# K's logarithm and exponential in one row on ScalarE, the next norm behind them, and the copy and subtraction of x behind those and behind Q's products

## The chip, the cores and the metric

The kernel runs on one core of a Trainium2 chip. The metric is device microseconds of one execution on that core. PE is TensorE (matmuls; PEld is its weight load), DVE is VectorE, ACT is ScalarE, POOL is GpSimd, SP is SyncE, which here issues transfers. Each engine takes its instructions strictly in the order in which they were issued to it; it waits where one of them needs something that another engine or a transfer has not yet delivered.

## The reference

```python
def _attn_ref(q, k, v, a_re, a_im):          # B, H, S, D = 4, 8, 768, 48
    mag = np.sqrt(a_re * a_re + a_im * a_im)
    scale = np.minimum(mag, 0.999) / (mag + 1e-06)
    a_re_n, a_im_n = (a_re * scale, a_im * scale)
    for t in range(S):
        ar, ai = (a_re_n[:, :, t, :, None], a_im_n[:, :, t, :, None])
        new_re = ar * S_re - ai * S_im
        new_im = ar * S_im + ai * S_re
        kv = np.einsum('bhd,bhe->bhde', k[:, :, t], v[:, :, t])
        S_re, S_im = (new_re + kv, new_im)
        y[:, :, t] = np.einsum('bhd,bhde->bhe', q[:, :, t], S_re)
...
def _moe_ref(x, domain_probs, w1, w2):       # 3072 tokens, width 384, 4 experts, hidden 1024
    p = domain_probs / (domain_probs.sum(-1, keepdims=True) + 1e-09)
    for e in range(E):
        h = np.maximum(x @ w1[e], 0.0)
        out += p[:, e:e + 1] * (h @ w2[e])
```

A linear attention whose state decays by a complex number per token and per row feeds a mixture of four experts: its output y, with the heads side by side, is the experts' input x.

## The kernel before

**Groups and blocks.** The 3072 tokens are cut into 12 groups of 256 (`NG`, `G`), each of two chunks of 128. The first part of the run (to about 585 us) does the attention of all groups and experts 0 and 1 of all groups; the second part does experts 2 and 3 from x in another matmul scheme. In the first part, block g-1 is `moe1(g-1)`: the experts of group g-1 in eight steps f2 = 0 to 7. A step makes `ph` (18 matmuls of 128x256, x times w1, at L238), copies it through the relu into `hh` on ACT (L249), takes the remainder `hl` on DVE (L250), and then makes `po` from both (8 matmuls with hh, 4 with hl, 128x384, at L261). All fp32 products are made from a high and a low half, so x too comes as two tiles: `xha`, a copy of x on ACT in the rounded type (L225), and `xla`, the difference of x and xha on DVE (L227). From group 3 on (`XSEL`), x is loaded from DRAM as `xa` (L218, issued by SP), after y went there in transfers that ACT issues (L704).

**What runs beside a block.** While PE works on block g-1, ACT and DVE prepare the attention of later groups. `stream()` yields, group after group, `front(g)` and then `norm(g+1)`:

- `norm(g)`: the magnitudes of the decay. Two squares on ACT (L389, L390), their sum on DVE (L391), logarithm, exponential, square and a linear function on ACT (L400, L401, L409, L411), then products on DVE (L410, L413, L416) and the scaling of A (L418).
- `front(g)`: the prefix products of A within the group, on DVE: tiles `pf` (seven steps over segments), `sk` (five doublings) and `fm` (four long products and the two lines that write A's real and imaginary half, L376 and L377). Then `head`: two squares of A on ACT (L488 real half, L489 imaginary half), for each of the two chunks a sum on DVE (L492), a logarithm (L494) and an exponential (L495) on ACT, and two products on DVE that make Q (L497). Then `tail`, on DVE: the products `u` (L512, L513, L514) and K (L516).
- `attention(g)`, also in pieces: K transposed (`ktp` on PE, copied to `KT` by ACT at L568), scores (`sc` on PE, masked to `scs` on DVE at L609), outputs (`yp` on PE, copied to y by ACT at L632), the state's increment (`dp` on PE, G on DVE at L597), `rotate` of the state (L644 to L647, tiles P and G on DVE), and the load of x.

So in block 2 (PE on group 2's experts) DVE takes K of group 3, norm(4), the scan of group 4 and then the head of group 4; x of group 3, which PE needs for block 3, arrives near the end of the block.

**What sets the order.** The pieces are emitted between the steps of a block (`between(k)`), as many as a paced budget allows. A scheduler then orders each engine's instructions by its own priorities. `behind(ins, prev)` adds that `ins` is issued after `prev` on the same engine; `tc.keep_in_program_order` keeps an instruction in the order of the code among those marked so. Scratch tiles named s and u belong to norm and to head and tail; st_a and st_m keep sums for a check at the end.

Of the kernel before, what the change touches and what calls it, by code (L numbers as in the profile page):

```python
# [10 lines left out]
AF = mybir.ActivationFunctionType  # L11
ALU = mybir.AluOpType
# [33 lines left out]
A2_LOG = (22, 58)  # L46
# [10 lines left out]
NSEL = 2  # L57
XSEL = 3
# [64 lines left out]
def fast_path(ctx, tc, qkP, aP, vP, probsP, w, out, flag):  # L123
    nc = tc.nc
# [93 lines left out]
        wts["xd"] = nc.sync.dma_start(x, y_d[g].rearrange("(j p) t -> p j t", p=P))  # L218
        return [(slice(0, G), x)]

    def split_x(g, parts):
        xh = moe.tile([P, NJ, G], F32R, tag="xh", name=f"xha{g}")
        xl = moe.tile([P, NJ, G], F32R, tag="xl", name=f"xla{g}")
        for ts, x in parts:
            ins = nc.scalar.activation(xh[:, :, ts], x, AF.Copy)  # L225
            tc.keep_in_program_order(ins)
            tc.keep_in_program_order(nc.vector.tensor_tensor(xl[:, :, ts], x, xh[:, :, ts], op=ALU.subtract))  # L227
        wts["x"] = ins
        return xh, xl

# [65 lines left out]
    with ExitStack() as c1:  # L296
# [82 lines left out]
        last = {}  # L379
# [82 lines left out]
        def finish(g, A, qk):  # L462
            s = tmp(f"s2{g}")
            u = tmp(f"u2{g}")
            Q = big.tile([P, 2, NR, C + 1], F32, tag="tmp", name=f"Q{g}", bufs=TMP)
            K = []

            def im(ap):
                return ap.rearrange("p (i m) -> p i m", i=SEG)

            def some(ap, lo, hi):
                if hi - lo == CG:
                    return ap.rearrange("p i m -> p (i m)")
                return ap.rearrange("p i (j c s) -> p i j c s", j=NJ, c=CG)[:, :, :, lo, :]

            def rows(ap, lo, hi):
                if hi - lo == CG:
                    return ap.rearrange("p i (n s) -> p i n s", s=CS)
                return some(ap, lo, hi)

            def dst(ap, lo, hi):
                x = ap.rearrange("p n (i s) -> p i n s", i=SEG)
                return x if hi - lo == CG else x[:, :, lo::CG, :]

            a2a, i0a, b2a, ta = im(s[:, 0]), im(u[:, 0]), im(s[:, 1]), im(u[:, 1])

            def head(lo, hi):
                nc.scalar.activation(some(a2a, lo, hi), some(A[:, 0], lo, hi), AF.Square)  # L488
                nc.scalar.activation(some(b2a, lo, hi), some(A[:, 1], lo, hi), AF.Square)  # L489
                for c in range(lo, hi):  # L490
                    a2, ic = some(a2a, c, c + 1), some(i0a, c, c + 1)
                    red = nc.vector.tensor_tensor_reduce(a2, a2, some(b2a, c, c + 1), scale=1.0, scalar=3e38,  # L492
                                                         op0=ALU.add, op1=ALU.min, accum_out=st_a2[:, c, g:g + 1])
                    nc.scalar.activation(ic, a2, AF.Ln, scale=2.0 ** A2_LOG[c], bias=a2b)  # L494
                    last_act = nc.scalar.activation(ic, ic, AF.Exp, scale=-1.0, bias=a2e[:, c:c + 1])  # L495
                for c in range(2):
                    ins = nc.vector.tensor_tensor(dst(Q[:, c, :, :C], lo, hi), rows(A[:, c], lo, hi),  # L497
                                                  rows(qk[:, 0], lo, hi), op=ALU.mult)
                    if g < NSEL and lo == 1:
                        behind(ins, red)  # L500
                        last["qp"] = ins
                if hi == CG:
                    nc.scalar.activation(Q[:, :, :, C].rearrange("p c (j n) -> p c j n", n=CG),
                                         A[:, :, SEG - 1, NS - 1::NS].unsqueeze(3).broadcast_to([P, 2, NJ, CG]),
                                         AF.Copy)
                return last_act

            def tail(lo, hi):
                if not K:
                    K.append(big.tile([P, 2, NR, C], F32, tag="K", name=f"K{g}", bufs=1))  # L510
                a2, i0, t, kn = (some(x, lo, hi) for x in (a2a, i0a, ta, qk[:, 1]))
                nc.vector.tensor_tensor(t, a2, i0, op=ALU.mult)  # L512
                nc.vector.scalar_tensor_tensor(t, t, 2.0, i0, op0=ALU.subtract, op1=ALU.mult)  # L513
                nc.vector.tensor_tensor(t, kn, t, op=ALU.mult)  # L514
                for c in range(2):
                    last_dve = nc.vector.tensor_tensor(dst(K[0][:, c], lo, hi), rows(A[:, c], lo, hi), rows(ta, lo, hi),  # L516
                                                       op=ALU.mult)
                return last_dve

            return Q, K, head, tail  # L520
# [367 lines left out]
        def stream():  # L888
            for g in range(1, NG):
# [7 lines left out]
                for r in front(g, A[g], qk):  # L897
                    yield g, r
                if g + 1 < NG:
                    for r in norm(g + 1, A[g + 1]):  # L900
                        yield g, r

        work = stream()
# [20 lines left out]
        for g in range(1, NG + 1):  # L924
# [7 lines left out]
            def between(k, g=g, first=first, end=end):  # L932
# [12 lines left out]
                    if k == end:  # L945
                        over.add(g)
                if k == max(end, nk - 1) and g in x and g >= NSEL:
                    x[g] = split_x(g, x[g])
                advance(STEP.get(g, 3.4) + (MORE[k - first] if first <= k <= end else 0.0), g + 1)

            moe1(g - 1, *x.pop(g - 1), between)
# [565 lines left out]
```

## Time and profile before

| | |
|---|---|
| median of 3 runs | 964.38 us (963.53 to 966.71) |
| the profiled execution, its own time | 963.93 us |
| its span | 962.2 us |
| PE busy | 935.6 us, 97% |
| DVE busy | 740.6 us, 77% |
| ACT busy | 480.2 us, 50% |

The time of an execution holds the span and what lies around it (1.73 us in the profiled one). Busy shares are means over the whole span; the first part and the second part differ, so a change is read from the stretch in which it lies.

### The profile page before, as it was taken

What the parts mean: (1) busy time and instruction counts of PE and PEld (TensorE: products, weight loads), DVE (VectorE), ACT (ScalarE), POOL (GpSimd) and SP (SyncE); (2) the same over time, 40 slices, a digit from 0 to 9 for tenths busy, and PEclk for the clock granted to TensorE, in tenths of its full rate; (3) what the DMA queues carried; (4) which work ended last, traced back from release to release, by engine and by line L of the source; (5) the groups of instructions that cost most, each with busy time, mean ns of one, the idle gap of its engine ahead of it and who ended that gap; (6) DMA issues with size and microseconds to landing.
All of it is one profiled execution on the core that took longest, in us unless ns stands there. A gap on an engine that the chain in (4) does not pass through costs nothing.

```text
span 962.2 us, 18383 instructions
## 1 busy us (share of the span) xinstructions
PE 935.6 (97%) x7037; PEld 912.9 (95%) x7037; DVE 740.6 (77%) x1640; ACT 480.2 (50%) x952; POOL 165.2 (17%) x206
## 2 busy tenths in 40 slices
PE   5899999999999999999999999999999999999997
PEld 3799999989999999999999999999999999999997
DVE  7889989988989999889895676758485757676642
ACT  7756436364464636446253455636454554444430
POOL 6020000000000000000000026333534362322000
PEclk9999999999999999999999999999999999999999
DMA  9686175674857468393949799231514443131112
GB/s 299 193 156 165 54 202 137 166 150 135 179 149 187 120 149 192 113 216 97 215 115 275 268 302 273 60 116 41 151 60 137 155 96 99 50 99 50 50 50 77
DMA packets 131459, 139.57 MB, mean 145 GB/s; under 512 B 8802, under 2 KB 115090, under 8 KB 131362
## 3 DMA queue, kind: packets, MB, share of 16 engines
q1 hardware_dynamic: 116130, 107.84, 38.9%
q0 software_dynamic: 11488, 26.93, 12.1%
q10 hardware_dynamic: 3744, 3.54, 1.4%
q8 instruction: 57, 0.93, 0.4%
q14 instruction: 40, 0.33, 0.1%
HBM read 89.80 MB, written 48.47 MB: 144 GB/s over the span
## 4 chain that ended last, share of the span: by engine, by line
PE 60%; DMA 3%; DVE 2%; ACT 1%; issue 0%; SPq 0%; DVEq 0%; ACTq 0%
PE pob L979 20%; PE pb L979 17%; PE po L261 9%; PE ph L238 9%; PE sc L604 2%; PE yp L621 1%; PE yp L626 1%; DMA RX<-w 1%; PE dp L586 1%; DMA Z<-y_d 1%; PE ktp L567 1%; DMA late_d<-lwl 0%; DMA xa<-y_d 0%; DVE lws L779 0%; DMA y_d<-y 0%
## 5 line engine op out<-in xcount | busy, mean ns | idle before, releaser
L979 PE MATMUL pob<-shi,hid 128*128 128x384 f32 x528 | 148.3, 334 | 0.0
L261 PE MATMUL po<-whi,hh 128*128 128x384 f32 x384 | 129.9, 338 | 1.4 <-ACT hh L249 1.0
L261 PE MATMUL po<-wlo,hh 128*128 128x384 f32 x384 | 128.7, 335 | 0.0
L249 ACT ACTIVATE hh<-ph 128x512 fp32r<-128x512 f32 x96 | 57.1, 595 | 132.0 <-PE ph L238 126.2
L991 POOL TENSOR_TENSOR Z<-Z 128x384 f32<-128x384 f32 x84 | 90.6, 1123 | 112.3 <-DMA Z<-y_d 47.9
L238 PE MATMUL ph<-xha,whi 128*128 128x256 f32 x576 | 103.3, 287 | 2.9 <-ACT xha L225 2.8
L238 PE MATMUL ph<-xla,whi 128*128 128x256 f32 x576 | 101.8, 284 | 0.6 <-DVE xla L227 0.6
L238 PE MATMUL ph<-xha,wlo 128*128 128x256 f32 x576 | 102.4, 284 | 0.0
L979 PE MATMUL pb<-xh,shi 128*128 128x384 f32 x291 | 97.2, 335 | 0.6 <-DVE pb L985 0.6
L979 PEld LDWEIGHTS pob<-shi,hid 128*128 128x128 f32 x528 | 96.4, 188 | 0.2 <-DVE hid L988 0.2
L979 PE MATMUL pb<-xh,slo 128*128 128x384 f32 x288 | 96.2, 334 | 0.0
L979 PE MATMUL pb<-xl,shi 128*128 128x384 f32 x288 | 96.2, 334 | 0.0
L250 DVE SCALAR_TENSOR_TENSOR hl<-ph,hh 128x512 fp32r<-128x512 f32 x96 | 66.0, 688 | 32.3 <-ACT hh L249 31.8
L238 PEld LDWEIGHTS ph<-xha,whi 128*128 128x128 f32 x576 | 85.1, 190 | 5.4 <-ACT xha L225 4.0
L979 PE MATMUL pob<-slo,hid 128*128 128x384 f32 x264 | 88.2, 334 | 0.0
L261 PE MATMUL po<-whi,hl 128*128 128x384 f32 x384 | 84.3, 336 | 0.0
L238 PEld LDWEIGHTS ph<-xla,whi 128*128 128x128 f32 x576 | 83.2, 190 | 1.1 <-DVE xla L227 0.8
L238 PEld LDWEIGHTS ph<-xha,wlo 128*128 128x128 f32 x576 | 82.7, 190 | 0.2 <-issue 0.2
L982 ACT ACTIVATE SN<-pb 128x384 f32<-128x384 f32 x96 | 47.3, 492 | 66.6 <-PE pb L979 59.2
L985 DVE TENSOR_TENSOR xl<-Z,xh 128x384 fp32r<-128x384 f32 x104 | 60.1, 607 | 21.1 <-ACT xh L982 13.3
L261 PEld LDWEIGHTS po<-whi,hh 128*128 128x128 f32 x384 | 72.4, 189 | 2.2 <-ACT hh L249 1.4
L982 ACT ACTIVATE hid<-pb 128x384 fp32r<-128x384 f32 x76 | 37.3, 490 | 72.3 <-PE pb L979 71.7
(227 smaller groups left out, 2069.6 us busy)
## 6 DMA issues: line engine op xcount, KB each, us to landing
qk<-qkP SPq DMA_DIRECT2D x24, 384.0 KB, 3.6
acc_d<-acc POOLq DMA_DIRECT2D x24, 384.0 KB, 4.8
ACC<-acc_d SPq DMA_DIRECT2D x48, 192.0 KB, 2.9
A<-aP SPq DMA_DIRECT2D x22, 384.0 KB, 5.5
k_d<-K SPq DMA_DIRECT2D x40, 192.0 KB, 4.1
Kst<-k_d SPq DMA_DIRECT2D x40, 192.0 KB, 5.7
Z<-y_d SPq DMA_DIRECT2D x16, 384.0 KB, 3.9
q_d<-Q SPq DMA_DIRECT2D x24, 193.5 KB, 3.7
```

The source lines that it names most:

```text
L238: ins = nc.tensor.matmul(ph[:, u, :], wt[:, j * P:(j + 1) * P], xt[:, j, :], start=(n == 0), stop=(n == 3 * NJ - 1))
L249: wts["hh"] = nc.scalar.activation(hh, ph, AF.Relu)
L250: wts["hl"] = nc.vector.scalar_tensor_tensor(hl, ph, 0.0, hh, op0=ALU.max, op1=ALU.subtract)
L261: ins = nc.tensor.matmul(po[t], part[0][:, u, t * P:(t + 1) * P], wts[i][n][:, HD:], start=(i % FE == 0 and part[0] is hh and n == 0), sto ...
L567: ins = nc.tensor.transpose(kt_ps[:, j * P:(j + 1) * P], K[0][:, i, j * CG + c, :], ident)
L586: ins = nc.tensor.matmul(d_ps[o:o + n, h, :], KT[:, h, o:o + n], vc[:, h * D:(h + 1) * D], start=True, stop=True)
L604: ins = nc.tensor.matmul(s_ps[:, h, :], Kc[:, hf * 4 + h, :], Qc[:, hf * 4 + h, :], start=True, stop=True)
L621: ins = nc.tensor.matmul(yo, st[:, o:o + n], Qc[:, o // D, :], start=True, stop=False)
L979: return tc.keep_in_program_order(nc.tensor.matmul(*args, **kw))
L982: return pin(nc.scalar.activation(dst, src, fn, scale=scale))
L985: pin(nc.vector.tensor_tensor(dst, x, y, op=op))
L991: nc.gpsimd.tensor_tensor(dst, x, y, op=op)
```

## The change

All of it takes effect from group 3 on. In `head`, the logarithm of the second chunk is issued behind the exponential of the first, so that ACT takes logarithm, exponential, logarithm, exponential. `norm(g+1)` gets what `norm(1)` already had: its two squares on ACT are issued behind the last exponential of `head(g)`, and its sum on DVE behind the last product of K. `split_x` issues the copy `xha` behind the last exponential of the newest head, and `xla` behind the last product for that head's Q. The newest head at that place in the code is that of the group after the one whose x is split: `xha` and `xla` of group 3 stand behind the exponentials and Q of group 4. No instruction is added or removed.

```diff
--- before.py
+++ after.py
@@ -218,13 +218,16 @@
         wts["xd"] = nc.sync.dma_start(x, y_d[g].rearrange("(j p) t -> p j t", p=P))
         return [(slice(0, G), x)]
 
-    def split_x(g, parts):
+    def split_x(g, parts, prev=(None, None)):
         xh = moe.tile([P, NJ, G], F32R, tag="xh", name=f"xha{g}")
         xl = moe.tile([P, NJ, G], F32R, tag="xl", name=f"xla{g}")
         for ts, x in parts:
             ins = nc.scalar.activation(xh[:, :, ts], x, AF.Copy)
             tc.keep_in_program_order(ins)
-            tc.keep_in_program_order(nc.vector.tensor_tensor(xl[:, :, ts], x, xh[:, :, ts], op=ALU.subtract))
+            low = tc.keep_in_program_order(nc.vector.tensor_tensor(xl[:, :, ts], x, xh[:, :, ts], op=ALU.subtract))
+            for later, p in zip((ins, low), prev):
+                if p is not None:
+                    behind(later, p)
         wts["x"] = ins
         return xh, xl
 
@@ -491,11 +494,14 @@
                     a2, ic = some(a2a, c, c + 1), some(i0a, c, c + 1)
                     red = nc.vector.tensor_tensor_reduce(a2, a2, some(b2a, c, c + 1), scale=1.0, scalar=3e38,
                                                          op0=ALU.add, op1=ALU.min, accum_out=st_a2[:, c, g:g + 1])
-                    nc.scalar.activation(ic, a2, AF.Ln, scale=2.0 ** A2_LOG[c], bias=a2b)
+                    ln = nc.scalar.activation(ic, a2, AF.Ln, scale=2.0 ** A2_LOG[c], bias=a2b)
+                    if g > NSEL and c > lo:
+                        behind(ln, last_act)
                     last_act = nc.scalar.activation(ic, ic, AF.Exp, scale=-1.0, bias=a2e[:, c:c + 1])
                 for c in range(2):
                     ins = nc.vector.tensor_tensor(dst(Q[:, c, :, :C], lo, hi), rows(A[:, c], lo, hi),
                                                   rows(qk[:, 0], lo, hi), op=ALU.mult)
+                    last["qm"] = ins
                     if g < NSEL and lo == 1:
                         behind(ins, red)
                         last["qp"] = ins
@@ -897,7 +903,8 @@
                 for r in front(g, A[g], qk):
                     yield g, r
                 if g + 1 < NG:
-                    for r in norm(g + 1, A[g + 1]):
+                    prev = (last["act"], last["dve"]) if g > NSEL else (None, None)
+                    for r in norm(g + 1, A[g + 1], prev=prev):
                         yield g, r
 
         work = stream()
@@ -945,7 +952,7 @@
                     if k == end:
                         over.add(g)
                 if k == max(end, nk - 1) and g in x and g >= NSEL:
-                    x[g] = split_x(g, x[g])
+                    x[g] = split_x(g, x[g], (last["act"], last["qm"]) if g >= XSEL else (None, None))
                 advance(STEP.get(g, 3.4) + (MORE[k - first] if first <= k <= end else 0.0), g + 1)
 
             moe1(g - 1, *x.pop(g - 1), between)
```

How the instructions stand then on the engines is shown at the end of block 2; lines of the changed kernel are three higher from L228 on (L249 is L252), six higher from L496 on (L568 is L574), and the head's logarithm and exponential are L497 and L500.

DVE, before, the end of group 4's scan (A_1530 is A of group 4, G_1_2350 the state of group 3, hl_6_2402 and hl_7_2463 the remainders of block 2's last two steps). The four doublings sk_1a to sk_8a all stand ahead of the first of these rows:

```order
L369 TENSOR_TENSOR sk_16a<-A_1530 128x2x48
L370 TENSOR_TENSOR sk_16a<-A_1530 128x2x48
L376 TENSOR_TENSOR A_1530<-sk_16a 128x3x16
L377 TENSOR_TENSOR A_1530<-sk_16a 128x3x16
L372 TENSOR_TENSOR fm_1a<-A_1530 128x651
L374 TENSOR_TENSOR fm_1a<-A_1530 128x651
L373 TENSOR_TENSOR fm_1b<-A_1530 128x651
L375 TENSOR_TENSOR fm_1b<-A_1530 128x651
L597 TENSOR_TENSOR G_1_2350<-G_0_2238,dp_1_2333 112x384
L250 SCALAR_TENSOR_TENSOR hl_6_2402<-ph_6_2382,hh_6_2401 128x512
L376 TENSOR_TENSOR A_1530<-fm_1a,fm_1b 128x21x31
L377 TENSOR_TENSOR A_1530<-fm_1a,fm_1b 128x21x31
```

DVE, after, from hl_6_2402 to the doubling sk_16a of the same group:

```order
L253 SCALAR_TENSOR_TENSOR hl_6_2402<-ph_6_2382,hh_6_2401 128x512
L652 TENSOR_TENSOR G_1_2350<-G_1_2350,TA 112x384
L372 TENSOR_TENSOR sk_4a<-A_1530 128x2x48
L373 TENSOR_TENSOR sk_4a<-A_1530 128x2x48
L653 TENSOR_TENSOR G_1_2350<-G_1_2350,P_157 112x384
L379 TENSOR_TENSOR A_1530<-sk_4a 128x12x4
L380 TENSOR_TENSOR A_1530<-sk_4a 128x12x4
L372 TENSOR_TENSOR sk_8a<-A_1530 128x2x48
L373 TENSOR_TENSOR sk_8a<-A_1530 128x2x48
L379 TENSOR_TENSOR A_1530<-sk_8a 128x6x8
L380 TENSOR_TENSOR A_1530<-sk_8a 128x6x8
L372 TENSOR_TENSOR sk_16a<-A_1530 128x2x48
```

and DVE, after, the rows that follow, to the first sum of the head:

```order
L373 TENSOR_TENSOR sk_16a<-A_1530 128x2x48
L253 SCALAR_TENSOR_TENSOR hl_7_2463<-ph_7_2443,hh_7_2462 128x512
L379 TENSOR_TENSOR A_1530<-sk_16a 128x3x16
L380 TENSOR_TENSOR A_1530<-sk_16a 128x3x16
L375 TENSOR_TENSOR fm_1a<-A_1530 128x651
L377 TENSOR_TENSOR fm_1a<-A_1530 128x651
L376 TENSOR_TENSOR fm_1b<-A_1530 128x651
L378 TENSOR_TENSOR fm_1b<-A_1530 128x651
L379 TENSOR_TENSOR A_1530<-fm_1a,fm_1b 128x21x31
L380 TENSOR_TENSOR A_1530<-fm_1a,fm_1b 128x21x31
L495 ISA s_2006,st_a_152<-s_2006 128x24x16
```

Before, hl_6_2402 comes once the doublings and the four fm products are through, just ahead of A's last two lines, and hl_7_2463 comes later; after, hl_6_2402 stands ahead of sk_4a, and hl_7_2463 ahead of the last line pair of sk_16a, so that the doublings sk_4a to sk_16a, the fm products and A's last lines all come behind hl_6_2402, and rotate's products on G among them.

ACT, before, the end of block 2 (xha_2417 is x of group 3, s_2006 and u_2007 belong to the head of group 4, s_2430 to norm(5)):

```order
L249 ACTIVATE hh_6_2401<-ph_6_2382 128x512
L225 ACTIVATE xha_2417<-xa_2354 128x768
L249 ACTIVATE hh_7_2462<-ph_7_2443 128x512
L488 ACTIVATE s_2006<-A_1530 128x768
L489 ACTIVATE s_2006<-A_1530 128x768
L494 ACTIVATE u_2007<-s_2006,a2b 128x24x16
L503 ACTIVATE Q_2008<-A_1530 128x12
L389 ACTIVATE s_2430<-A_2003 128x768
L390 ACTIVATE s_2430<-A_2003 128x768
L249 ACTIVATE hh_0_2516<-ph_0_2497 128x512
L494 ACTIVATE u_2007<-s_2006,a2b 128x24x16
L495 ACTIVATE u_2007<-u_2007,a2e 128x24x16
```

ACT, after, the same place:

```order
L252 ACTIVATE hh_6_2401<-ph_6_2382 128x512
L252 ACTIVATE hh_7_2462<-ph_7_2443 128x512
L749 ACTIVATE acc_1_2532<-po_4_0_2208,pr 128x384
L749 ACTIVATE acc_1_2532<-po_4_1_2209,pr 128x384
L491 ACTIVATE s_2006<-A_1530 128x768
L492 ACTIVATE s_2006<-A_1530 128x768
L497 ACTIVATE u_2007<-s_2006,a2b 128x24x16
L509 ACTIVATE Q_2008<-A_1530 128x12
L500 ACTIVATE u_2007<-u_2007,a2e 128x24x16
L497 ACTIVATE u_2007<-s_2006,a2b 128x24x16
L500 ACTIVATE u_2007<-u_2007,a2e 128x24x16
L225 ACTIVATE xha_2417<-xa_2354 128x768
```

Before, xha_2417 stands right behind hh_6_2401 and ahead of all of group 4's head; after, it stands behind that head's squares, logarithms and exponentials, and the squares of norm(5) (L392, L393) follow it.

PE, before, where block 3 begins (ph_0_2497 and ph_1_2554 are block 3's first steps):

```order
L261 MATMUL po_4_0_2208<-whi_602,hl_6_2402 128x384
L261 MATMUL po_4_1_2209<-whi_602,hl_6_2402 128x384
L238 MATMUL ph_0_2497<-xha_2417,whi_502 128x256 x3
L238 MATMUL ph_0_2497<-xha_2417,wlo_503 128x256 x3
L261 MATMUL po_4_0_2208<-whi_604,hh_7_2462 128x384
L261 MATMUL po_4_0_2208<-wlo_824,hh_7_2462 128x384
L261 MATMUL po_4_1_2209<-whi_604,hh_7_2462 128x384
L261 MATMUL po_4_1_2209<-wlo_824,hh_7_2462 128x384
L261 MATMUL po_4_0_2208<-whi_606,hh_7_2462 128x384
L261 MATMUL po_4_0_2208<-wlo_827,hh_7_2462 128x384
L261 MATMUL po_4_1_2209<-whi_606,hh_7_2462 128x384
L261 MATMUL po_4_1_2209<-wlo_827,hh_7_2462 128x384
```

PE, after, the same place:

```order
L264 MATMUL po_4_0_2208<-whi_604,hl_7_2463 128x384
L264 MATMUL po_4_1_2209<-whi_604,hl_7_2463 128x384
L264 MATMUL po_4_0_2208<-whi_606,hl_7_2463 128x384
L264 MATMUL po_4_1_2209<-whi_606,hl_7_2463 128x384
L241 MATMUL ph_0_2497<-xha_2417,whi_502 128x256 x3
L241 MATMUL ph_0_2497<-xha_2417,wlo_503 128x256 x3
L241 MATMUL ph_1_2554<-xha_2417,whi_524 128x256 x3
L241 MATMUL ph_1_2554<-xha_2417,wlo_525 128x256 x3
L241 MATMUL ph_0_2497<-xla_2418,whi_502 128x256 x3
L241 MATMUL ph_0_2497<-xha_2417,whi_513 128x256 x3
L241 MATMUL ph_0_2497<-xha_2417,wlo_514 128x256 x3
L241 MATMUL ph_0_2497<-xla_2418,whi_513 128x256 x3
```

Before, the first six matmuls with xha_2417 stand ahead of block 2's last step (hh_7_2462); after, all of block 2's po matmuls come first, and then block 3 begins, twelve matmuls with xha_2417 ahead of the first with xla_2418.

## Rows read from the trace of the kernel before

**Rows 1.** The head of the page of the kernel before: the span, and for each engine the busy time, its share of the span and the instructions.

```profile
span 962.2 us, 18383 instructions
...
PE 935.6 (97%) x7037; PEld 912.9 (95%) x7037; DVE 740.6 (77%) x1640; ACT 480.2 (50%) x952; POOL 165.2 (17%) x206
```

**Rows 2.** Windows: one row for a stretch, with its length, the busy time of PE, PEld, DVE, ACT and POOL (x instructions), the granted clock of TensorE as a share of full speed, the DMA share and GB/s. The first stretch holds the end of block 2, the second the rest of the first part.

```profile
155.00:194.00 39.00, 37.68 (x348) 36.67 (x346) 35.05 (x81) 18.43 (x35) 0.57 (x1) 1.00 0.62 163
194.00:600.00 406.00, 403.75 (x3473) 394.45 (x3473) 340.30 (x784) 205.33 (x386) 32.29 (x42) 1.00 0.69 185
```

**Rows 3.** Timeline of all engines round the end of block 2: start, duration, engine, line, operation, out<-in, shapes and count; in brackets the idle time before it and what ended that.

```profile
190.43 0.34 PE L261 MATMUL po<-whi,hh 128*128 128x384 f32 x1
...
191.82 0.86 PE L261 MATMUL po<-whi,hl 128*128 128x384 f32 x4
193.38 0.84 ACT L225 ACTIVATE xha<-xa 128x768 fp32r<-128x768 f32 x1 [4.92 <-DMA xa<-y_d]
194.25 0.96 DVE L227 TENSOR_TENSOR xla<-xa,xha 128x768 fp32r<-128x768 f32 x1 [1.88 <-ACT xha L225]
...
194.27 0.62 PE L238 MATMUL ph<-xha,whi 128*128 128x256 f32 x3 [1.59 <-ACT xha L225]
```

**Rows 4.** Timeline of ACT (and of the queue in which it issues, ACTq) before group 2's hh_6.

```profile
185.80 1.95 ACTq L704 DMA_DIRECT2D y_d<-y  x2
187.85 0.60 ACT L249 ACTIVATE hh<-ph 128x512 fp32r<-128x512 f32 x1 [1.47 <-issue]
```

**Rows 5.** Timeline of DVE at the end of group 4's prefix scan, in the order of the kernel before.

```profile
183.24 0.26 DVE L369 TENSOR_TENSOR sk_4a<-A 128x96 f32<-128x96 f32 x1
...
185.59 0.83 DVE L372 TENSOR_TENSOR fm_1a<-A 128x651 f32<-128x651 f32 x1
...
188.59 0.55 DVE L597 TENSOR_TENSOR G<-G,dp 112x384 f32<-112x384 f32 x1
189.05 0.68 DVE L250 SCALAR_TENSOR_TENSOR hl<-ph,hh 128x512 fp32r<-128x512 f32 x1
189.65 0.83 DVE L376 TENSOR_TENSOR A<-fm_1a,fm_1b 128x651 f32<-128x651 f32 x1
190.40 0.83 DVE L377 TENSOR_TENSOR A<-fm_1a,fm_1b 128x651 f32<-128x651 f32 x1
191.26 0.55 DVE L644 TENSOR_TENSOR P<-G,TB 48x384 f32<-48x384 f32 x1
```

**Rows 6.** Timeline of DVE at K of group 3 and norm(4).

```profile
157.98 0.95 DVE L391 CUSTOM_DVE_ANT_0 s<-s 128x768 f32<-128x768 f32 x1
...
158.93 1.06 DVE L512 TENSOR_TENSOR u<-s,u 128x384 f32<-128x384 f32 x2
...
163.34 0.95 DVE L410 TENSOR_TENSOR u<-s,u 128x768 f32<-128x768 f32 x1
164.21 1.02 DVE L516 TENSOR_TENSOR K<-A,u 128x384 f32<-128x384 f32 x2
165.14 0.69 DVE L250 SCALAR_TENSOR_TENSOR hl<-ph,hh 128x512 fp32r<-128x512 f32 x1
```

**Rows 7.** Timeline of ACT at norm(4) (L400 logarithm, L401 exponential, L409 square) and at the copies of KT behind it.

```profile
159.78 0.93 ACT L400 ACTIVATE s<-s,m2b 128x768 f32<-128x768 f32 x1
160.75 0.94 ACT L401 ACTIVATE s<-s,lnb 128x768 f32<-128x768 f32 x1
161.72 0.85 ACT L409 ACTIVATE u<-s 128x768 f32<-128x768 f32 x1
...
166.84 0.87 ACT L568 ACTIVATE KT<-ktp 128x384 f32<-128x384 f32 x2 [2.88 <-PE ktp L567]
```

**Rows 8.** Waits of DVE between norm(4) and the end of group 4's scan: what waited for what, us in total, times, the longest.

```profile
DVE scs L609 <- PE sc L604: 1.4, 2, 1.0
DVE hl L250 <- ACT hh L249: 0.2, 1, 0.2
```

**Rows 9.** Timeline of ACT at a head whose logarithm follows its squares (group 6).

```profile
278.31 0.85 ACT L489 ACTIVATE s<-A 128x768 f32<-128x768 f32 x1
...
279.79 0.62 ACT L494 ACTIVATE u<-s,a2b 128x384 f32<-128x384 f32 x1
```

**Rows 10.** Windows of 2.81, 0.72, 3.41 and 1.60 us, with the columns of Rows 2: a pause of PE early in the kernel, the 0.72 us after it, the 3.41 us after those, and the pause at the end of block 2.

```profile
24.35:27.16 2.81, 0.00 (x0) 0.00 (x0) 2.11 (x7) 1.92 (x5) 0.00 (x0) 1.00 1.08 373
27.16:27.88 0.72, 0.72 (x8) 0.66 (x10) 0.72 (x3) 0.69 (x2) 0.00 (x0) 1.00 1.16 410
27.88:31.29 3.41, 3.41 (x34) 3.34 (x31) 3.36 (x10) 0.87 (x3) 0.00 (x0) 0.50 0.54 187
...
192.60:194.20 1.60, 0.08 (x1) 0.00 (x0) 0.00 (x0) 0.82 (x2) 0.00 (x0) 1.00 0.09 31
```

**Rows 11.** Timeline of PE where block 3 meets block 4.

```profile
241.95 0.52 PE L238 MATMUL ph<-xla,whi 128*128 128x256 f32 x3
243.14 0.45 PE L261 MATMUL po<-whi,hh 128*128 128x384 f32 x1 [0.67 <-ACT hh L249]
```

**Rows 12.** Timeline of ACT at the head of group 5 and at the two copies of x that follow, those of groups 4 and 5.

```profile
234.79 0.84 ACT L489 ACTIVATE s<-A 128x768 f32<-128x768 f32 x1
238.67 0.85 ACT L225 ACTIVATE xha<-xa 128x768 fp32r<-128x768 f32 x1 [3.04 <-DMA xa<-y_d]
...
284.01 0.84 ACT L225 ACTIVATE xha<-xa 128x768 fp32r<-128x768 f32 x1 [1.01 <-DMA xa<-y_d]
```

## The prediction

> **What bounds the kernel now.** I read the engines' shares first: PE is busy for 935.6 of 962.2 us [rows 1], so a change can save only what PE still waits. The windows say where that is: PE is idle for 39.00 - 37.68 = 1.32 us of the stretch that ends at 194 and for 406.00 - 403.75 = 2.25 us from 194 to 600 [rows 2]. The change acts only between these marks, so 3.57 us is the most it can give back. What it can cost is not so bounded. DVE is busy for 340.30 of 406.00 us there, 84% [rows 2], and in the stretch before for 35.05 of 39.00: a stop of DVE's is not caught up quickly.
>
> The timeline at the end of block 2 shows PE's longest wait in the stretch that changes [rows 3]. The last four po matmuls start at 191.82 and take 0.70 us from start to free engine (four of 0.174, as the eight from 190.43 to 191.82), so PE is free at 192.5 and starts block 3 at 194.27: 1.75 us. It waited for xha, which had waited for the transfer of x (ACT starts it at 193.38, after 4.92 us of idleness). xha to PE's start takes 0.89. So x of group 3 is already the last thing to arrive at this boundary, and whatever makes xha later moves PE.
>
> **The copy of x, step by step.** After the change xha of group 3 stands behind the whole head of group 4 on ACT, and the head needs A of group 4, which DVE makes. So the question is when DVE delivers A. DVE takes its work in the new order, in which hl_6 stands ahead of sk_4, and needs hh_6. hh_6 is written by ACT from 187.85 to 188.45, held up to then by the two sends of y (they occupy ACT's queue from 185.80 for 1.95 us, and the idle time of 1.47 before hh_6 is put down to issue) [rows 4]. That order of ACT is unchanged. So hl_6 starts at 188.45 at the earliest, here called T.
>
> What DVE must still do from T to A's real half, by the rows of before [rows 5]: hl_6 0.60 (189.05 to 189.65); the doublings sk_4 to sk_16, 2.35 (183.24 to 185.59); the two lines of rotate on G, as one such line on G (188.59 to 189.05), 2 x 0.46 = 0.92, of which some fills gaps between the doublings; hl_7 0.60; the four fm products, 3.00 (185.59 to 188.59); and A's real half 0.75 (189.65 to 190.40). Together 8.2. In before, all but 1.35 of it was done by then. So A's real half is there at 196.7, the first square starts at about 196.8, the second 0.75 later at 197.55.
>
> Then the head. From the second square's start to the first logarithm 1.48 (278.31 to 279.79) [rows 9]; then logarithm, exponential, logarithm, exponential, about 0.55 each with the small copy between them, 2.2; so xha starts at 197.55 + 1.48 + 2.2 = 201.2 and PE 0.89 later at 202.1. PE's own work lets it be there earlier: in the new order block 2's last step comes first, so it is free at 192.5 + 1.39 (eight with hh_7) + 0.70 (four with hl_7) = 194.6. The wait becomes 7.5 us in place of 1.75: **+5.75**. Twelve matmuls with xha lie ahead of the first with xla; xla comes behind Q and four products u on DVE, some 2 us after xha, so 0.0 to 0.5 more: I take 0.1.
>
> **The hold on the norm.** The sum of norm(4) moves from 157.98 to behind K. K of group 3 takes DVE 163.34 - 158.93 = 4.41 with one hl in it, and 0.93 (164.21 to 165.14) for the rest [rows 6]; begun 0.95 earlier it ends at 163.3, the sum at 164.3. Only then comes the logarithm, and exponential and square 0.97 after each other [rows 7], with KT's copies between them now. Without these the square ends at 164.3 + 1.94 + 0.85 = 167.1; if they come as late as before (166.84, 0.44 each), the square begins at 168.7 and ends at 169.5. So DVE, which has one hl (0.60) to do meanwhile, waits 2.2 to 4.6 us before norm's first product; I take 3.6, to 168.5. From there to hl_6: before, it is 189.05 - 163.34 = 25.71; less K's rest 0.93, hl_3 0.60, the fm products 3.00, the doublings 2.35 and the waits of 1.6 [rows 8], plus two lines of P, 2 x 0.55: 18.3. That reaches hl_6 at 186.8, or at 187.8 by the later bound: before T. So this stop **costs 0**, because the wait for hh_6 at T covers it; the cover is 0.6 to 3 us, and beyond it each us would be one of PE's.
>
> **The clock.** A pause of 2.81 us before 27.16 was followed, 0.72 us later, by 3.41 us at a granted clock of 0.50, that is 1.2 GHz in place of 2.4; the pause of 1.60 at this boundary left the clock at 1.00 [rows 10]. A wait of 7.5 is well over the first. The stretch at half clock held 34 matmuls in 3.41 us, 0.100 each, and the one before it 8 in 0.72, 0.090 each: by that 34 x 0.010 = 0.35 would be lost, since those matmuls were not back to back. Here they are, and twice the time for each would cost half of 3.41, 1.7. I take **+1.3**, nearer to the end that back-to-back work is like. The Trainium skill ("TensorE: Matmul & The Clock Gate", Part 1: The HAM clock gate) says that the array drops to 1.2 GHz after it has idled and comes back only after sustained work; by that the fall comes within the wait and the whole stretch runs slow, a sum 0.4 higher; the row at 27.16 had its fall only after work had begun again.
>
> **What comes back.** At the next boundary PE waited for hh_7, which stood on ACT behind xha, two squares and three logarithms and exponentials: from 241.95 + 0.36 = 242.31 to 243.14, 0.83 [rows 11]. The new order has only the norm's squares between xha and hh_7: **-0.8**. The other waits of the 2.25 are each under 0.5; I count nothing for them, and at most 1.2.
>
> **Later boundaries.** They cost nothing, I think. The copies of x of groups 4 and 5 start at 238.67 and 284.01, both when the transfer lands [rows 12]. A head has to end before. In before's places the second squares are at 234.79 and 278.31 [rows 9, 12]; 1.48 + 2.2 later is 238.5 and 282.0. The cover is 0.2 and 2.0 us there; it grows, because after the first boundary PE is later by 8 and DVE, whose head was done while PE waited, by some 6 less 2 to 4 of new norm wait. Over a block DVE needs 84% of the time, so it has about 7 us to absorb the norm's stop. The second part of the run, after 600, is untouched.
>
> **The sum.** 963.93 (the profiled execution's own time) + 5.75 + 0.1 + 1.3 - 0.8 = 970.3. That execution is 0.45 below the median of the runs, so against the median 964.38 the time is 970.7.
>
> **Rivals.** *More*: the stop before norm's product recurs in eight norms, and if the cover of 0.2 at the boundary of groups 3 and 4 stays thin, DVE is late there and after. For it: DVE at 84%, and the sends of y stand behind the next head's first square in that block, so a late A makes x late too. Against it: the slack of 7 us a block. Half of the seven later boundaries losing 2 us gives 970.7 + 7 = 978.
>
> *Same*: the terms at their lower ends. If hl_6 does not wait (hh_6 written 1.5 earlier, as the idle time before it allows), DVE reaches it at 186.8 and PE waits 5.85; no clock loss beyond 0.35; and all of 2.0 comes back: 964.38 + 4.1 + 0.35 - 2.0 = 966.8. Against it: hh_6's place behind the sends is unchanged.
>
> *Faster*: the one mechanism is PE's waits themselves. With po ahead of ph at the boundary PE has 2.1 us more to do before it needs x, so if the head is through by 193.7, no wait is left there, and the waits for hh go as well: 964.38 - 3.57 = 960.8. The point that decides is A's real half at 189.2 or sooner; before had it at 190.4 and the new order has 8.2 us of DVE's work behind a row at 188.45. That speaks nearly shut.
>
> **How the numbers follow.** A measurement of this kernel tells 0.3% (2.9 us) from no change. Forecast, with DVE's order setting xha, 0.66, its own range 967.5 to 974; more 0.10; same 0.17; faster 0.07. So faster by over 0.3% (below 961.5) 0.06, within 0.24 (the rest of these two and the forecast's lowest values), slower 0.70. The range for 8 in 10 goes from 965.0, with most of the same case, to 975.5: the clock at 1.7, KT late and 2 us lost at one later boundary.
>
> **What would show it.** Right: between 194.6 and 202 PE idle for some 7 us, ended by ACT's copy xha; a granted clock of 0.50 for 3 us at about 202; DVE waiting 2 to 4 us for the square of norm(4) near 165 to 169, and waiting for hh_6 at about 188; head of group 4 starting at 196.8; PE's wait for hh_7 at the next boundary gone; x of later groups copied when its transfer lands. Wrong: A of group 4 done by 191, or a wait for xha at later boundaries that the transfer does not end.

## The result, and the profile after

The changed kernel takes 974.12 us (median of 5 runs, 972.26 to 975.51) against 964.38 us: a ratio of 1.0095, 95% interval 1.0078 to 1.0112. It is slower by 9.7 us, where 6.3 were forecast and the range reached to 975.5. The profiled execution took 975.51 us, the slowest of the five and 1.4 above that median, so the sums below, made from its rows, come to somewhat more than the medians differ by: its span is 973.4 against 962.2, +11.2 us.

The head of the page after, for [rows 1], and the two windows of [rows 2]:

```profile
span 973.4 us, 18385 instructions
...
PE 936.5 (96%) x7037; PEld 912.6 (94%) x7037; DVE 743.0 (76%) x1640; ACT 480.9 (49%) x952; POOL 164.9 (17%) x206
```

```profile
155.00:194.00 39.00, 38.78 (x356) 37.99 (x355) 33.82 (x79) 18.46 (x35) 0.57 (x1) 1.00 0.65 163
194.00:600.00 406.00, 394.36 (x3404) 384.33 (x3403) 336.68 (x770) 197.26 (x366) 26.29 (x35) 0.99 0.67 177
```

PE's busy time is nearly the same (936.5 us against 935.6) in a longer span. Up to 194 it waits less than before, since the boundary of blocks 2 and 3 now lies behind that mark; from 194 to 600 its idle time is 406.00 - 394.36 = 11.64 us, where it was 2.25.

The end of block 2, for [rows 3]: timeline of all engines.

```profile
193.90 0.86 PE L264 MATMUL po<-whi,hl 128*128 128x384 f32 x4
...
200.63 0.83 ACT L225 ACTIVATE xha<-xa 128x768 fp32r<-128x768 f32 x1
...
201.51 1.01 PE L241 MATMUL ph<-xha,whi 128*128 128x256 f32 x3 [6.75 <-ACT xha L225]
```

PE is through with block 2 at 193.90 + 0.70 = 194.6, and starts block 3 at 201.51. In front of it stands ACT's copy xha, which now begins at 200.63, 7.25 us later than before. That is not because x landed late: the copy follows ACT's work ahead of it without a pause, and x was sent for at 189.56 and takes 3.0 to 3.3 us to land. How that came about shows on ACT, for [rows 4, 9], and on DVE, for [rows 5, 6]:

```profile
185.09 0.93 ACTq L710 DMA_DIRECT2D y_d<-y  x2
186.40 0.60 ACT L252 ACTIVATE hh<-ph 128x512 fp32r<-128x512 f32 x1 [0.72 <-PE ph L241]
...
196.08 0.84 ACT L491 ACTIVATE s<-A 128x768 f32<-128x768 f32 x1 [0.41 <-DVE A L379]
```

```profile
163.38 0.95 DVE L394 CUSTOM_DVE_ANT_0 s<-s 128x768 f32<-128x768 f32 x1
...
164.25 0.69 DVE L253 SCALAR_TENSOR_TENSOR hl<-ph,hh 128x512 fp32r<-128x512 f32 x1
168.34 0.96 DVE L413 TENSOR_TENSOR u<-s,u 128x768 f32<-128x768 f32 x1 [3.40 <-ACT u L412]
...
187.79 0.69 DVE L253 SCALAR_TENSOR_TENSOR hl<-ph,hh 128x512 fp32r<-128x512 f32 x1
...
195.21 0.84 DVE L379 TENSOR_TENSOR A<-fm_1a,fm_1b 128x651 f32<-128x651 f32 x1
```

On DVE the sum of norm(4) (L394) stands behind K; then there is one hl, and then DVE stops for 3.40 us, until ACT has made logarithm, exponential and square (L412 writes u), with KT's two copies between them. The head of group 4 starts when DVE has made A's real half (195.21), at 196.08. The rows of hl_6 and hh_6 carry a surprise: the two sends of y began 0.7 us earlier and took 0.93 us, not 1.95 (the second took 0.31, not 1.33), hh_6 was written at 187.00, and hl_6 began at 187.79 without a wait.

The clock behind that wait, for [rows 10]: windows with the granted clock in the third column from the end.

```profile
194.42:201.33 6.91, 0.34 (x2) 0.02 (x1) 5.97 (x12) 5.63 (x10) 0.85 (x1) 0.91 0.50 88
201.33:206.50 5.17, 4.99 (x23) 4.99 (x24) 5.17 (x11) 1.59 (x3) 0.00 (x0) 0.50 0.76 206
206.50:207.00 0.50, 0.50 (x5) 0.50 (x4) 0.42 (x2) 0.00 (x0) 0.00 (x0) 0.64 1.15 302
207.00:208.00 1.00, 1.00 (x10) 1.00 (x10) 0.34 (x1) 0.97 (x2) 0.00 (x0) 1.00 1.09 312
```

PE resumes at 1.2 GHz: the granted clock is 0.50 for some 5.4 us, from PE's start at 201.51 to about 206.9, and 1.00 behind that. The mean of 0.91 over the wait says that the fall came within it. What that costs shows on four rows of PE, two at half clock and two at full:

```profile
202.31 0.84 PE L241 MATMUL ph<-xha,wlo 128*128 128x256 f32 x3
202.95 0.84 PE L241 MATMUL ph<-xha,whi 128*128 128x256 f32 x3
...
207.55 0.52 PE L241 MATMUL ph<-xha,wlo 128*128 128x256 f32 x3
207.91 0.53 PE L241 MATMUL ph<-xla,whi 128*128 128x256 f32 x3
```

At half clock the next three matmuls start 0.64 us later, at full clock 0.36. So 0.28 of each 0.64 us is lost, which makes about 2.4 us in the 5.4.

Last, what PE (from 155 to the end of the first part) and DVE (from 155 to 560) waited for: us in total, times, the longest. PE before, then PE after, then DVE after:

```profile
PE ph L238 <- ACT xha L225: 1.6, 1, 1.6
PE po L261 <- ACT hh L249: 1.0, 2, 0.7
PE po L261 <- ACT acc L743: 0.4, 1, 0.4
```

```profile
PE ph L241 <- ACT xha L225: 7.4, 2, 6.7
PE sc L610 <- DMA Kst<-k_d: 2.1, 1, 2.1
PE sc L610 <- issue: 1.4, 2, 1.2
PE po L264 <- DVE hl L253: 0.8, 1, 0.8
```

```profile
DVE u L413 <- ACT u L412: 14.8, 8, 3.4
...
DVE xla L227 <- ACT xha L225: 1.0, 1, 1.0
```

PE's 3.0 us of waits have become 11.7. Of the 7.4 for xha, 6.7 are the wait above and the rest is one at the last boundary, where ACT itself waits 3.6 us for the transfer of x. Of the others, 2.1 stand at scores whose K arrives late by its transfer (Kst), 1.4 at other scores, for which the profile shows no releaser (`issue`), and 0.8 at one hl. The waits for hh and acc of before are gone. With the half clock this is 11.7 - 3.0 + 2.4 = 11.1, against 11.2 by the spans. And DVE stops 14.8 us in eight norms for what the first stop shows; for xha it hardly waits.

### The profile page after: what moved, and what is told of

It reads as the page before. It is cut to its first block, busy times and chain, and to the rows that moved or that the text cites. A ratio compares the mean times of both kernels' runs of the same rounds, so it can differ in the third digit from the quotient of the medians.

```text
span 973.4 us, 18385 instructions
## 1 busy us (share of the span) xinstructions
PE 936.5 (96%) x7037; PEld 912.6 (94%) x7037; DVE 743.0 (76%) x1640; ACT 480.9 (49%) x952; POOL 164.9 (17%) x206
## 4 chain that ended last, share of the span: by engine, by line
PE 83%; DVE 7%; DMA 4%; ACT 3%; issue 1%; SPq 0%; DVEq 0%; ACTq 0%
PE pob L986 20%; PE ph L241 18%; PE pb L986 17%; PE po L264 16%; PE sc L610 4%; PE dp L592 2%; PE yp L632 2%; PE yp L627 2%; PE ktp L573 1%; DMA lw<-w 1%; DMA wst<-w 1%; DMA y_d<-y 1%; PE xp L662 1%; DMA Kst<-k_d 1%; DVE hl L253 1%
## 5 line engine op out<-in xcount | busy, mean ns | idle before, releaser
L252 ACT ACTIVATE hh<-ph 128x512 fp32r<-128x512 f32 x96 | 57.3, 597 | 137.2 <-PE ph L241 136.8
L241 PE MATMUL ph<-xha,whi 128*128 128x256 f32 x576 | 105.5, 290 | 8.6 <-ACT xha L225 8.6
L241 PEld LDWEIGHTS ph<-xha,whi 128*128 128x128 f32 x576 | 86.6, 192 | 11.2 <-ACT xha L225 9.9
```

What stands on the lines that cost most here:

```text
L241: ins = nc.tensor.matmul(ph[:, u, :], wt[:, j * P:(j + 1) * P], xt[:, j, :], start=(n == 0), stop=(n == 3 * NJ - 1))
L252: wts["hh"] = nc.scalar.activation(hh, ph, AF.Relu)
```

## The experiments

Each ratio is to the kernel before on the same chip, with its 95% interval; the medians of before in the three sets of runs were 965.68, 964.80 and 965.10 us, and 965.42 for the last run. Two theories stood against each other: that the hold on x makes the loss, at the first boundary, and that the stop of DVE in the norm makes it. Each edit frees or adds an order between a few instructions; the scheduler then orders the rest anew, and other instructions move too (with the norm's sum free, KT's copies on ACT and `ktp` on PE stand elsewhere, for instance). What a run shows is a hold together with the order that follows from it.

**Without the hold on x.**

```diff
-  x[g] = split_x(g, x[g], (last["act"], last["qm"]) if g >= XSEL else (None, None))
+  x[g] = split_x(g, x[g])
```

> The changed kernel without the hold on xha and xla; the order of logarithm and exponential and the hold on the norm stay. If the hold on x is the cause: PE's wait of 6.91 us at the end of block 2 goes back to about 1.75, the clock stays at 1.00 there, and the time is 964 to 966. If the stop of DVE before the norm's first product (14.8 us in eight norms) is the cause: the wait at the end of block 2 shrinks, but the waits for the scores of later groups (1.3 and 2.3 us) stay, and the time is 967 to 970.

Measured: 994.81 us, ratio 1.0284 (1.0260 to 1.0307). Neither theory had this: taking the hold on x alone out of the change makes it some 19 us slower still. Waits of DVE, and of PE for xha:

```profile
DVE u L413 <- ACT u L412: 26.6, 8, 3.6
DVE xla L227 <- ACT xha L225: 16.6, 6, 4.4
```

```profile
PE ph L241 <- ACT xha L225: 17.8, 7, 11.6
```

The stop in the norm has grown to 26.6 us, and 16.6 us of waiting for xha have come beside it, since xla now stands on DVE ahead of the head and waits there for x. Together this is 43 us in eight groups. By these waits DVE now sets the pace of a block, and PE waits at seven boundaries, for 17.8 us. So within the change the hold on x saves DVE's time, and the hold on the norm is what needs it.

**The hold on the norm alone** (neither x held nor the logarithms in one row) settles that:

```diff
-  if g > NSEL and c > lo:
+  if False:
...
-  x[g] = split_x(g, x[g], (last["act"], last["qm"]) if g >= XSEL else (None, None))
+  x[g] = split_x(g, x[g])
```

> The hold on the norm alone: x is free, logarithms and exponentials as before. If the stop before the norm's product, added to DVE's waits for xha, makes DVE the engine that sets the pace of a block: as slow as without the hold on x, 990 to 998, with waits of DVE for the norm's square of 20 us and more. If the order of logarithm and exponential was part of that loss: clearly less, under 985.

Measured: 995.12 us, 1.0314 (1.0298 to 1.0330), with 26.9 us of DVE's waits for the norm's square. The hold on the norm by itself costs 3%, and the row of logarithms has no part in that which these two runs could show (their intervals overlap).

**Without the hold on the norm**, x held:

```diff
-  prev = (last["act"], last["dve"]) if g > NSEL else (None, None)
+  prev = (None, None)
```

> The changed kernel without the hold on the norm; x is held. If the wait at the end of block 2 is set by what stands between the scores of group 3 and group 4's head on DVE, the stop of 3.4 us before the norm's product is mostly covered: PE still waits 6 to 7 us there, the clock still falls, and only the later waits (for the scores and the last boundary, some 5 us) can go: 969 to 972. If that stop is what makes the head late, PE waits 3.5 us at most, the clock stays at 1.00, and the time is 965 or less.

Measured: 969.96 us, 1.0042 (1.0030 to 1.0054). Waits of PE:

```profile
PE ph L241 <- ACT xha L225: 5.6, 2, 5.1
PE sc L610 <- issue: 0.9, 1, 0.9
```

The later waits for Kst and for hl are gone, and a wait for xha of 5.1 us at the end of block 2 stays, with a half clock behind it (0.54 over the 3.3 us after it). That is less than the 6 to 7 that I expected and more than 3.5: without the stop in the norm the first wait is 1.6 us shorter, and most of the later ones are gone.

**The hold on x alone**, without the row of logarithms (both the edit above and the `if False`):

> The hold on xha and xla alone: neither the order of logarithm and exponential nor the hold on the norm. If the first hold of x costs a wait once and the norm's stop makes the rest: PE waits 5 us at the end of block 2, nothing after that, and the ratio to before is that of the kernel without the norm's hold (1.004), 968 to 971. If the order of logarithm and exponential matters for the head's length, the wait at the end of block 2 is longer than 5.3 us.

Measured: 969.62 us, 1.0056 (1.0041 to 1.0071), PE's longest wait for xha 4.3 us. The interval overlaps with that of the run before it.

**The row of logarithm and exponential alone** (x and norm free):

> The order logarithm, exponential, logarithm, exponential alone. It moves at most four instructions of ACT by 0.6 us each per group, and ACT is busy for half of the time: within 0.2% of before, 964 to 967, no wait of PE over 2 us.

Measured: 965.25 us, 1.0001 (0.9990 to 1.0012): no difference.

**x of group 3 free, x of groups 4 to 11 held**, with the rest of the change:

```diff
-  ... if g >= XSEL else (None, None))
+  ... if g > XSEL else (None, None))
```

> The changed kernel with x of group 3 not held, x of groups 4 to 11 held as in the change. If the loss is made at the first boundary and the holds on later x are covered by the transfer of x: 5.2 us of waiting and 2.7 us of half clock go, 966. If the later holds delay PE as well: the time stays above 969, and PE waits for xha at a later boundary.

Measured: 977.28 us, 1.0107 (1.0090 to 1.0124), as slow as the whole change. Timeline of PE at the two boundaries, and windows at the second:

```profile
193.67 0.62 PE L241 MATMUL ph<-xha,whi 128*128 128x256 f32 x3 [0.87 <-ACT xha L225]
...
249.54 0.79 PE L241 MATMUL ph<-xha,whi 128*128 128x256 f32 x2 [6.51 <-ACT xha L225]
```

```profile
242.70:249.30 6.60, 0.34 (x2) 0.01 (x1) 5.66 (x11) 5.57 (x10) 0.85 (x1) 0.74 0.54 89
249.30:252.00 2.70, 2.46 (x11) 2.46 (x12) 2.70 (x6) 1.66 (x3) 0.00 (x0) 0.50 1.02 258
```

The wait is not gone; it has moved. At the end of block 2 PE now waits for 0.9 us, and at the end of block 3, the first where x is held, for 6.5, with the half clock behind it. So moving the first hold by one group moves the wait. I read it so: the hold puts the whole next head ahead of x, so DVE has to be further ahead of PE than it was, and PE stands still until it is; after that the lead is there. The changed kernel fits this: one boundary behind its standstill the head is through, and ACT waits 1.88 us for x's transfer before it copies x at 246.11. The run with the first hold at group 5, below, shows a place where the first hold costs nothing.

**Spare matmuls in the wait.** With the whole change, 48 matmuls whose result is not used, between the last of block 2 and the first of block 3:

```diff
+                        wts["w2"] = ins
...
+                if b == 3 and f2 == 0:
+                    self.flush()
+                    spare = ps_a.tile([P, G], F32, tag="pa", name="spare")
+                    for n in range(48):
+                        prev = nc.tensor.matmul(spare, wts[0][0][:, :P], wts[0][0][:, P:P + G],
+                                                start=(n == 0), stop=(n == 47))
+                        if n == 0:
+                            behind(prev, wts["w2"])
```

> The changed kernel with 48 spare matmuls of 128x256 (about 5.8 us at full clock, their result is not used) on PE between the last matmul of block 2 and the first of block 3, where PE waits 6.91 us for xha. If the fall of the clock behind that wait costs 2.7 us (half of 5.35 us at 0.50): the granted clock stays at 1.00 and the time falls by 2 to 3, to 971.5. If it costs what I forecast, 1.3: 972.8. If the clock is not what costs there: 974, the wait for xha being the same.

Measured: 973.60 us, 1.0077 (1.0058 to 1.0095). Timeline of PE, a window of what follows, and the row of the changed kernel with the same matmuls of K (`ktp`):

```profile
194.85 5.91 PE L291 MATMUL spare<-whi 128*128 128x256 f32 x48
201.77 0.50 PE L241 MATMUL ph<-xha,whi 128*128 128x256 f32 x2 [1.02 <-ACT xha L225]
...
206.52 0.71 PE L582 MATMUL ktp<-wide,K 128*128 128x128 f32 x5
```

```profile
201.70:205.00 3.30, 3.14 (x24) 2.94 (x25) 3.30 (x7) 1.49 (x3) 0.00 (x0) 1.00 0.91 230
```

```profile
208.27 0.81 PE L573 MATMUL ktp<-wide,K 128*128 128x128 f32 x6
```

The clock stays at 1.00 (in the rest of the wait too), and PE goes on with block 3 at 201.77, 0.26 later than in the changed kernel. From there to the first `ktp`, 36 matmuls of block 3, it takes 206.52 - 201.77 = 4.75 us, 0.25 of it a pause for xla; in the changed kernel the same 36 take 208.27 - 201.51 = 6.76. So the half clock cost 2.0 us between these two executions, and 2.3 if that pause is left out. The spans differ by more, 971.0 against 973.4, but those of the changed kernel alone reach from 970.2 to 973.4; the ratios differ by 0.0018, 1.7 us, and their intervals overlap. The size rests on the rows.

**Half of the norm's hold.** First the squares held and the sum free, x held as in the change:

```diff
-  prev = (last["act"], last["dve"]) if g > NSEL else (None, None)
+  prev = (last["act"], None) if g > NSEL else (None, None)
```

> The changed kernel with half of the norm's hold: its two squares on ACT stay behind the last exponential, its sum on DVE is free. If the stop of DVE comes from the sum being last in the row (sum, logarithm, exponential, square, with only one hl beside them): the sum goes ahead of K's products, which then cover ACT's three steps; the waits of DVE for the norm's square fall from 14.8 us to under 3, and the time is that of the kernel without the norm's hold, ratio 1.003 to 1.006. If the squares on ACT make the norm late: 1.009 as with the whole change.

Measured: 966.68 us, 1.0016 (1.0007 to 1.0026), less than the 1.003 expected at least. Timeline of DVE at norm(4), DVE's waits for the norm's square, and PE's for xha:

```profile
160.15 0.96 DVE L394 CUSTOM_DVE_ANT_0 s<-s 128x768 f32<-128x768 f32 x1 [0.15 <-ACT s L393]
...
163.04 1.96 DVE L522 TENSOR_TENSOR K<-A,u 128x384 f32<-128x384 f32 x4
164.92 0.95 DVE L413 TENSOR_TENSOR u<-s,u 128x768 f32<-128x768 f32 x1
```

```profile
DVE u L413 <- ACT u L412: 2.6, 3, 1.0
```

```profile
PE ph L241 <- ACT xha L225: 3.3, 1, 3.3
```

The sum (160.15) now stands ahead of K's last products (163.04), and the norm's first product follows them at 164.92 without a wait: K covers what ACT does in between. The stops fall from 14.8 to 2.6 us, PE's wait for xha to 3.3, and it waits for nothing else until the second part.

Then the sum held and the squares free (`(None, last["dve"])`):

> The changed kernel with the other half: the norm's sum on DVE stays behind the last product of K, its squares on ACT are free. If the sum's place makes the stop: DVE still waits 12 us and more for the norm's square, ratio 1.008 to 1.011. If the squares do: 1.004.

Measured: 978.00 us, 1.0129 (1.0107 to 1.0150), DVE's waits for the norm's square 15.3 us, PE's for xha 8.6. That is above the 1.011 expected at most. So with the rest of the change in place, freeing the norm's sum takes away most of the loss (1.0095 to 1.0016), and what is left of PE's waits is the one at the first hold of x. The hold on the squares is a gain: with the sum free the ratio is 1.0016 with it and 1.0042 without (the run without the hold on the norm), clear of the intervals; with the sum held it is 1.0095 and 1.0129, where they overlap a little.

**x held from group 5 on**, norm free (`g > XSEL + 1` and the norm's edit above):

> No hold on the norm, the row of logarithm and exponential, and x held from group 5 on. If the first hold costs PE a wait wherever it is put, because the head of the next group is not yet through when x lands: 3 us and more at the boundary of blocks 4 and 5, 967 to 970. If the head is through by then, as the rows of before say of group 6 (second square at 278.31, x lands at 284.01), the hold is covered, DVE waits less for xha than the 6.4 us of before, and the time is 963 to 966.

Measured: 964.99 us, 1.0005 (0.9996 to 1.0014): PE does not wait for xha at the first boundary with a hold. ACT at that copy, and PE at the start of block 5:

```profile
284.16 0.84 ACT L225 ACTIVATE xha<-xa 128x768 fp32r<-128x768 f32 x1
```

```profile
287.13 0.52 PE L241 MATMUL ph<-xha,whi 128*128 128x256 f32 x3
```

The copy starts right behind the head's last exponential, about when x lands (sent for at 280.75, 3.2 us or more to landing), and not 2.0 us ahead of it, as the prediction had it from [rows 9, 12]. The hold costs nothing there because the copy is through at 285.0 and PE has block 4's last step to do until 287.13.

**The cheap parts together**: the row, the norm's squares held and its sum free, x held from group 5 on.

> The row of logarithm and exponential, the norm's squares held and its sum free, x held from group 5 on: the parts of the change that cost least, put together. If nothing of them stands on the path: within 0.2% of before. If the first hold of x costs only at the boundary of blocks 2 and 3 and what comes back at later boundaries stays: PE's waits between 155 and 600 fall from 3.6 to under 2.5 us and the time is 1 to 2 us under that of before.

Measured: 962.07 us (961.66 to 962.30), ratio 0.9965 (0.9953 to 0.9978): faster than before. The windows of [rows 2], and PE's waits:

```profile
155.00:194.00 39.00, 38.26 (x352) 37.07 (x350) 35.63 (x83) 18.44 (x36) 0.57 (x1) 1.00 0.68 165
194.00:600.00 406.00, 405.03 (x3484) 396.57 (x3485) 343.14 (x787) 208.28 (x390) 34.38 (x45) 1.00 0.69 186
```

```profile
PE ph L241 <- ACT xha L225: 1.3, 1, 1.3
```

PE is idle for 0.74 + 0.97 = 1.71 us, where before it was 3.57; the waits for hh and acc are gone, and only the one for x of group 3, which lands when it does, is left. By the profiled spans (960.4 against 962.2) this is 1.8 us; the medians say 2.1 to 4.5, and what the rest is, if there is one, the profiles don't show.

## Why the prediction was right in sign and range

**The first wait: right.** Forecast were A's real half through at 196.7, the head's first square at 196.8, xha at 201.2, PE at 202.1 and free from 194.6. Measured: 196.05, 196.08, 200.63, 201.51, and 194.6. The wait is 6.9 where 7.5 was forecast.

**Its reason: partly wrong.** The step "hl_6 starts at 188.45 at the earliest" failed: the sends of y began earlier and took half the time, hh_6 was there at 187.00, and DVE came to hl_6 at 187.79 by its own work. With that the next step fell too, that the norm's stop "costs 0, because the wait for hh_6 at T covers it". The stop itself was right (3.40 us, forecast 3.6, first product at 168.34, forecast 168.5), but without it PE waited 5.1 in place of 6.7, and with the norm's sum alone freed 3.3. Two errors of about one microsecond met: DVE's own way to hl_6, forecast to end at 186.8, took one more, with waits for scores (0.39 at 179.35) and an hh, and so ended near the floor that was not one. That the first wait came out so near its forecast is in that part luck.

**The clock: too small.** The step that took 3.41 us of half clock from an earlier place and priced it at 1.3 was too small in both: the stretch lasted 5.4 us and cost some 2.4. Its lower bound of 0.35 was a misreading of [rows 10]. The same early matmuls, before and after:

```profile
27.16 4.52 PE L457 MATMUL qp<-Q,wide 128*64 128x128 f32 x40 [2.81 <-DVE Q L497]
```

```profile
27.14 2.85 PE L460 MATMUL qp<-Q,wide 128*64 128x128 f32 x40 [2.67 <-DVE Q L502]
```

In the changed kernel's execution the clock stays at 1.00 there, and the same 40 matmuls take 2.85 us in place of 4.52: the stretch of 3.41 had cost PE 1.67, near the 1.7 of the back-to-back end. (This is also why PE's busy time hardly grew: one half-clock stretch came and another went.) The Trainium skill ("TensorE: Matmul & The Clock Gate", Part 1: The HAM clock gate) has the fall come with idleness and the return with sustained work; the trace agrees in both, with a mean of 0.91 in the wait and 5.4 us of work before 1.00 came back. Not every trace has the fall within the pause: with the squares held and the sum free the wait itself ran at 1.00, and the fall came after PE had begun again.

**What comes back: more than forecast.** Not only the 0.83 of [rows 11] but the waits for hh and acc altogether, 1.4 us by the views of waits.

**"Later boundaries cost nothing": wrong.** It held for x, but for the last boundary (7.4 - 6.7 = 0.7, where x itself landed late). It did not for K: 2.1 for Kst, 1.4 at other scores and 0.8 at an hl, 5.0 in all with the 0.7. The claim that DVE "has about 7 us to absorb the norm's stop" took idle time for spare time. My reading is that much of DVE's idle time before was itself waiting in a fixed order, and that the stop adds to it; no run takes these waits apart. The runs without the stop, with x held, have none of the waits for Kst and hl. The rival *more* named this mechanism and put it at the wrong place, x in place of K, with 7 us for 5.

So the forecast of +6.3 was made of 5.85 + 1.3 - 0.8, and the profiled +11.2 of 5.1 + 5.0 + 2.4 - 1.4 = 11.1: a first term close to its size, a clock nearly twice as dear, and a term of 5 us that had been set to nothing; what came back made up for a part. The time of 974.1 lies in the range, but at its upper end, which the prediction had reserved for a dearer clock, a late KT and 2 us lost at a later boundary. The two other rivals fell with the first wait.

## What to carry to other kernels

A reduction that starts a chain on another engine (here sum, logarithm, exponential, square) belongs ahead of the independent work that can cover the chain, not behind it: freeing that one instruction per group, with the order that followed from it, took the loss from 0.95% to 0.16%. A hold that makes an operand wait for the next stage's work asks for a lead of the producer. Where that lead was missing here, it was paid as one standstill, which moved when the first hold moved, and with a stretch at half clock behind it; where PE still had work of its own to do, the first hold cost nothing. Idle time of an engine that runs in a fixed order is not slack until one has looked at what each idle piece waits for.

## What the runs showed of the hardware

The stretch at 1.2 GHz behind a pause was 5.4 us long here and 3.41 in [rows 10], and matmuls of 128x256 took 0.21 us each in it against 0.12 at full clock. The waits of PE for the first held x, 3.3 to 8.6 us long in the six runs that had one with nothing put into it, each had such a stretch behind them; the pause of 1.60 in [rows 10], the 2.13 for Kst and the 1.02 behind the spare matmuls had none. A pause of nearly the same length went either way: 2.81 us early in the kernel before had the stretch, 2.67 at the same place of the changed kernel had not. And the fall can come after PE has resumed, as with the squares held and the sum free (the wait and the 1.55 us behind it; the next 2.00 us have 0.50):

```profile
194.93:198.40 3.47, 0.34 (x2) 0.02 (x1) 3.17 (x6) 3.24 (x6) 0.85 (x1) 1.00 0.48 133
198.45:200.00 1.55, 1.38 (x9) 1.38 (x10) 1.55 (x3) 1.55 (x3) 0.00 (x0) 0.83 1.09 156
```

The same two sends of y occupied ACT's queue for 1.95 us before and for 0.93 in the changed kernel, and before hh_6 stood idle behind them for 1.47 us.
